# A fused attention, mixture-of-experts and gated-convolution kernel: a re-made instruction list, masks first, half-height masks, divided bursts, tail projections in column halves

## The chip, the core and the metric

The kernel runs on one core of one Trainium2 chip. The time is the device time of one execution in microseconds (us). Several executions are timed and the median is compared. One further execution is taken by the hardware profiler; its trace is the source of every row below. The engines are TensorE (PE, with its weight loads on a track of their own, PEld), VectorE (DVE), ScalarE (ACT), GpSimd (POOL) and SyncE (SP), which here issues the DMAs.

## What is computed

Three stages for 4 batches of 576 positions:

```python
# 1: 8 heads of width 64; heads 0-3 look at the last 32 positions, heads 4-7 at every 32nd
mask_local   = (rel >= 0) & (rel < 32)
mask_strided = (rel >= 0) & (pos[None, :] % 32 == pos[:, None] % 32)
x = softmax(where(mask, q @ k.T / 8, -1e9)) @ v          # laid out as (4, 576, 512)
# 2: 4 experts, each a causal attention of head width 64; a gate keeps 2 of 4 per position
for e in range(4):
    y += gate[e] * (softmax(causal((x @ wq[e]) @ (x @ wk[e]).T / 8)) @ (x @ wv[e]) @ wo[e])
# 3: 512 -> 1024, relu, a 3-tap convolution along positions as gate, 1024 -> 512
h = relu(y @ w_in);  out = (h * sigmoid(conv3(h))) @ w_out
```

## The kernel before

**Number formats.** Products of stages 2 and 3 are made of float16 pairs: each operand is a high part and a low part (what the high part leaves), and `mm3` (L129) issues three products: high by high, low by high, high by low. A low part is made by `low` (L260): TensorE subtracts the high part inside PSUM with a scaled negative identity (`idn`), and ScalarE copies what is left. Stage 1 is in float32, and so is one product of weights: wo and w_in have no nonlinearity between them, so `w_wp` (L747) multiplies them into one matrix `wp` in the prologue (16 float32 products, L758).

**Stage 1** (`s1_local` L297, `s1_strided` L368). One course is a batch's pair of heads: 8 local and 8 strided courses. Each writes its scores by many tiny products (36 of 64x64 for a local, 64 of 64x18 for a strided; in float32 each shows as two records), after two products that lay the mask down (`m_sel` by `m_loc` or `m_str`, L236). A softmax of six DVE steps and one on ACT follows (L243), then a DVE transpose, copies of blocks into block-diagonal tiles (`cp`, L116: one engine each, by the table `ENG`, L71: `bd` alternates ACT and POOL, `bu` is all ACT) and the products with the values (L349, L410).

**Stage 2.** `p_v` (L429) projects the values and the gate's logits, one tile of 128 positions at a time and a last of 64; `p_qk` (L485) projects queries and keys; `a_unit` (L510) is a block of causal attention. It first lays the triangle of the mask into PSUM with two products of full height (`eye` by `m_c`, L521), one for each of two heads; the scores themselves are products of half height (64 rows).

**Stage 3.** `m_gate` (L597) and `m_out` (L633); the last batch ends in `m_last` (L657).

**Order.** All of it is cut into Python generators, one for each piece of work, in nine families: L loads, S stage-1 courses, W weights, O parts of w_out, V, Q, A, M, N. `ORDER` (L38) is a list of 1,669 pairs of letter and number; each pair advances one generator to its next `yield`. The order of the instructions on every engine and queue follows from it, and each engine takes its instructions in that order. The list loop stands under `tc.manual_schedule()` (L809); what comes before it in the function (memsets, masks, identities) is ordered by the framework. All loads go through SP's queue in list order; w_out goes through POOL's.

Of the kernel before, what the change touches and what calls it, by code (L numbers as in the profile page):

```python
# [23 lines left out]
X_S = 2.0 ** 5  # L24
# [9 lines left out]
PF_BUFS = 4  # L34
ST_BUFS = 4
# [3 lines left out]
    "W0W0W0W0W0L0L0L0L0L0W4W5W4W4W4W4W4S0S0S0W4W4S1W4L1L1L1L1L1S2W0S0S0W3S1W3S0L2S1L2S1S0L2S2S0S0S0S0L0S0W3S2S2L2L2S1"  # L39
    "S3S2W3L0L0W4S3S0S0S1W0S3S1S4S4W2S4S0W1W3W3S2S1S1S1S0S1S3W3S0S1S2W2S0S1S1S1S3S1S4W2S2W2W2W2S4S3W2S2S2S3S0S0S0S4W2"  # L40
    "S0S2S0W2S2S1S1L0L0L0L0S0S1S3W2S3S0W2W2S1S1W2W2W2W1W1W0W1W0S0W1W0W0W2L0S1S0S0L0W2W2W2S0S0S0S0S0W2S1S1S0L0S0S0W1S1"
    "S0V0V0W3V1W2W2W2W2V1V1L0W1S0S1W3L0L0L0L0V1W4W3W3V1S0S0S0W2W0W1W0W2W1W0W0W1L0L0W2W1W1S0S1Q0S0W0S1V1W0L0S0S0S1L0S0"
    "W1W1S1S1W1S0S0S0W0S1W0W0S1O0O1O1O1Q0Q0O0O0O0Q0O1V0O2O4V0S1Q0S1V0S2S2S2L0L0S0S0O1V2V0L0S1O1O0O1V0O2S2O1S2O1V0V1V2"
    "O0V2V2S0S0S1O1Q1Q1Q1Q1O6Q1Q0V2S0S0O0Q0Q0S1S0V1Q0V2S0S0A0A0A1A1Q0S0S0S0A0A0V2V2O4A0O1O1A1A1A0L0L0Q0A1A0A0O0S0S0A2"
    "S0V0A2A1A1S0S0Q0Q0A0A0A1O1A4V1A1A1A2O0A2A1A4A4V2A3O0A2A4A3Q0V0V1V1O1V1O0A4A2A0Q0Q0V0A2A2A4A1A1S0O1A3V0A4A2S1A2A2"
    "S0A1A2A0A2A3A0S0A3L1L1A2L1A2A2A2Q0A0Q0A2Q0A1Q0A2A0Q0Q0A2A2A2V0A0A0S1Q0A2A2A1A0S0A3V0O0V1A2L0A2A3A3S0O2A2L1L1A3V0"
    "V1V1S0A2A2A3S0A4A4V0A2A3V0V0S0V0S0L0A5S0A0S1S0A1Q0A2A2A2A0A3S0A5A4A1A3A4A1A2A2Q0S0Q0A0A1V0A3A2A3A4S2A2A2L0A0O1A3"
    "A3V0S1A2A2A2A4A4S2S2A4L0A0S0S0Q0A3A3A4A4S2S1Q2A0Q0Q2S1A3A3A3S0Q0A0V1S0Q0S1V0A3S0S0S0A2A2S1S0S0S0Q1S0S0S0S0Q0Q0V1"
    "O0Q0Q0O1V0Q0A3S1A3S0S0Q0A2A2O1O1Q0O0S0S0S0A4Q0V0A4A4A3O1A3A4Q0S1A2S1Q1V0S0O0V0V0L0O0Q0A0L0Q1L0S1Q0Q0O0O0S0S0A0S0"
    "S1O0O1A0V0A3A1A2A2Q0Q0A3O0A3A2O0S0A1A1S0A3A1A1A2A0O0A0Q0Q0A0A0S0A0S0A2A2O1O0O0M0M0A2A2M0M0M0M0M0S0A2A2M0S0M1O0S0"  # L50
# [820 lines left out]
```

## Time and profile before

| | us |
|---|---|
| median of 3 runs | 386.27 |
| their range | 385.08 to 389.83 |
| the profiled execution | 391.51 |
| its span, first to last instruction | 389.8 |

The profile names for each instruction its start, its length, the line, the operation and the tiles; in brackets stands how long the engine had been idle and what ended that. "issue" there means that the engine waited for nothing that the profile shows. PE's lengths overlap (products are pipelined), so the spacing of starts tells the cost of one. [...]

### The profile page before, as it was taken

The numbers are of one execution on the slowest core, as the hardware profiler recorded it, in microseconds if no ns is written. First come the engines' busy times: TensorE is split into PE (matmuls) and PEld (weight loads), VectorE is DVE, ScalarE is ACT, GpSimd is POOL, SyncE is SP. The second block draws the span as 40 slices with busy tenths as digits, with TensorE's granted clock in tenths as the row PEclk, the third lists the DMA queues.
The fourth block names the chain that finished last, engine by engine and source line by source line (L and its number), as shares of the span: only waits on it lengthen the run. The fifth ranks groups of instructions, "written<-read, shape, count | busy, mean of one in ns | idle before, by whom it ended". The sixth has DMA issues, their size and how long they took to land.

```text
span 389.8 us, 12020 instructions
## 1 busy us (share of the span) xinstructions
PE 355.6 (91%) x4948; PEld 237.4 (61%) x4948; DVE 304.5 (78%) x706; ACT 283.0 (73%) x643; POOL 30.4 (8%) x81
## 2 busy tenths in 40 slices
PE   3249998799999799999999899999999999999994
PEld 2236565666677567777556667777454687655442
DVE  7979996789889679999977766988957489848730
ACT  3357856689899589999587689988875788556532
POOL 4312113020001101000101010000000000000000
PEclk9759999699999889999999999999999999999999
DMA  8993876732955903324874582115169460010004
GB/s 281 323 245 102 225 249 173 279 111 56 222 119 112 137 9 119 78 41 97 202 128 95 116 129 67 29 21 84 33 154 161 121 129 16 0 69 29 0 2 149
DMA packets 79207, 45.91 MB, mean 118 GB/s; under 512 B 63792, under 2 KB 72496, under 8 KB 79152
## 3 DMA queue, kind: packets, MB, share of 16 engines
q1 hardware_dynamic: 78000, 40.94, 44.8%
q0 software_dynamic: 1152, 4.19, 3.0%
q8 instruction: 39, 0.64, 0.7%
q14 instruction: 16, 0.13, 0.1%
HBM read 25.20 MB, written 4.72 MB: 77 GB/s over the span
## 4 chain that ended last, share of the span: by engine, by line
PE 77%; issue 6%; DMA 6%; ACT 6%; DVE 3%; SPq 1%; ACTq 0%; POOLq 0%
PE o L650 14%; PE zav L584 6%; PE oe L650 5%; PE asc L526 5%; PE psq L130 4%; PE psq L131 4%; PE psq L132 4%; PE hps L130 4%; PE hps L132 3%; PE hps L131 3%; PE wps L758 3%; DMA apt<-pn 3%; PE av L349 3%; PE psv L130 2%; PE scs L240 2%
## 5 line engine op out<-in xcount | busy, mean ns | idle before, releaser
L650 PE MATMUL o<-wout,hs 128*128 128x512 f16 x288 | 66.1, 380 | 0.0
L650 PEld LDWEIGHTS <-hs 128*128 128x128 f16 x384 | 36.0, 98 | 42.5 <-issue 1.8
L619 DVE SCALAR_TENSOR_TENSOR t<-hs,taps,t 128x576 f32<-128x576 f32 x64 | 49.4, 818 | 6.9 <-ACT t L124 6.9
L124 ACT ACTIVATE pn<-apf,aden 64x64 f16<-64x64 f32 (+4 forms) x80 | 42.2, 558 | 12.4 <-DMA apt<-pn 6.9
L570 DVE SCALAR_TENSOR_TENSOR pn<-apf,aden,pn 128x320 f16<-128x320 f32 (+4 forms) x80 | 42.5, 549 | 7.5 <-ACT pn L124 7.3
L130 PE MATMUL psq<-xt,wqk 128*128 128x288 f16 x128 | 38.0, 297 | 0.0
L131 PE MATMUL psq<-xt,wqk 128*128 128x288 f16 x128 | 37.7, 295 | 0.0
L132 PE MATMUL psq<-xt,wqk 128*128 128x288 f16 x128 | 37.7, 295 | 0.0
L130 PE MATMUL hps<-z,wp 128*128 128x288 f16 x128 | 36.8, 288 | 0.0
L131 PE MATMUL hps<-z,wp 128*128 128x288 f16 x128 | 36.6, 286 | 0.0
L132 PE MATMUL hps<-z,wp 128*128 128x288 f16 x128 | 36.6, 286 | 0.0
L550 ACT ACTIVATE apf<-asc,anm 64x64 f32<-64x64 f32 (+3 forms) x64 | 29.8, 470 | 5.4 <-DVE anm L535 2.6
L584 PE MATMUL zav<-apt,v 128*64 128x128 f16 (+2 forms) x720 | 30.8, 221 | 1.4 <-ACT ob L124 1.0
L584 PEld LDWEIGHTS <-v 128*64 128x64 f16 (+1 forms) x720 | 22.7, 108 | 11.5 <-issue 7.2
L534 DVE TENSOR_REDUCE anm<-asc 64x2 f32<-64x128 f32 (+3 forms) x32 | 21.8, 681 | 6.1 <-PE asc L526 5.9
L124 ACT ACTIVATE qk<-psq 128x576 f16<-128x576 f32 x32 | 20.3, 641 | 8.5 <-PE psq L132 4.5
L127 DVE TENSOR_TENSOR hs<-t,hs 128x1152 f16<-128x1152 f32 x16 | 21.6, 1352 | 5.5 <-ACT hs L124 5.5
L124 ACT ACTIVATE t<-hs,taps 128x576 f32<-128x576 f32 x32 | 23.7, 772 | 1.0 <-DVE hs L127 1.0
L124 ACT ACTIVATE hs<-t 128x1152 f16<-128x1152 f32 x16 | 18.7, 1171 | 7.3 <-DVE t L625 7.3
L625 DVE SCALAR_TENSOR_TENSOR t<-t,hs 128x1152 f32<-128x1152 f32 x16 | 21.6, 1352 | 3.0 <-ACT t L623 2.9
L611 ACT ACTIVATE hs<-hps 128x576 f32<-128x576 f32 x32 | 20.4, 644 | 4.6 <-POOL hs L610 3.6
L130 PE MATMUL psv<-wvg,xt 128*128 128x260 f16 (+1 forms) x80 | 23.0, 287 | 0.0
(156 smaller groups left out, 786.2 us busy)
## 6 DMA issues: line engine op xcount, KB each, us to landing
st<-in_dram SPq DMA_DIRECT2D x8, 512.0 KB
ow<-in_dram POOLq DMA_DIRECT2D x8, 512.0 KB, 5.2
out_dram<-ob SPq DMA_DIRECT2D x16, 256.0 KB
ul<-in_dram SPq DMA_DIRECT2D x12, 288.0 KB
ul<-in_dram SPq DMA_DIRECT2D x12, 252.0 KB
vs<-in_dram SPq DMA_DIRECT2D x16, 144.0 KB
vn<-in_dram SPq DMA_DIRECT2D x8, 256.0 KB
st<-in_dram SPq DMA_DIRECT2D x4, 386.0 KB
```

The costliest lines, as they stand in the source:

```text
L124: act.activation(out=out, in_=in_, func=ACTF.Copy, scale=scale)
L127: eng.tensor_tensor(out=out, in0=a, in1=b, op=ALU.subtract)
L130: nc.tensor.matmul(out=out, lhsT=ah, rhs=bh, start=first, stop=False)
L131: nc.tensor.matmul(out=out, lhsT=al, rhs=bh, start=False, stop=False)
L132: nc.tensor.matmul(out=out, lhsT=ah, rhs=bl, start=False, stop=last)
L534: dve.tensor_reduce(out=nm[:, 0], in_=asc[:rows, :, :w], axis=mybir.AxisListType.X, op=ALU.max)
L550: act.activation(out=pfs[par], in_=scs[par], func=ACTF.Exp, scale=C2, bias=nm[:, 0, par:par + 1], accum_out=den[:, par:par + 1])
L570: dve.scalar_tensor_tensor(out=pn[:, 1, :w], in0=pfs[par], scalar=den[:, par:par + 1], in1=pn[:, 0, :w], op0=ALU.mult, op1=ALU.subtract)
L584: nc.tensor.matmul(out=av[64 * par:64 * par + 64, 0:rows], lhsT=v2[a][:kk, kb, D * e:D * e + D], rhs=pts[par][:kk, l, kb], start=(kb == 0 ...
L619: dve.scalar_tensor_tensor(out=t_[:, i], in0=tap, scalar=w, in1=t_[:, i], op0=ALU.mult, op1=ALU.add)
L625: dve.scalar_tensor_tensor(out=t_, in0=t_, scalar=1.0, in1=hs[:, :, 1:S + 1], op0=ALU.add, op1=ALU.mult)
L650: nc.tensor.matmul(out=ps, lhsT=g[a], rhs=wout[l][:, f], **at)
```

## The change

1. **The list** is made again (1,739 pairs); the whole function, prologue included, stands under `manual_schedule`, so masks and memsets come in the order in which they are written. The copies of the masks to the upper half are moved up behind each mask; the zeroing of the spare stage-1 set moves from DVE to POOL.
2. **Divided bursts.** The scores of a course may be left after every 8 jobs (`SCORES`), and the local products with the values after blocks 1 and 3 (`SPLIT_AV`).
3. **Half-height masks.** The triangle in `a_unit` is laid by products of 64 rows, one pair for each 64 columns.
4. **Tail projections in column halves.** The last tile of `p_v` (64 positions) is 24 products of half the columns, the two halves on the two halves of TensorE's columns.
5. **Low parts** of some pieces are made by one DVE instruction from PSUM instead of a product and an ACT copy (table `LOW`: 4 of 16 in x, 2 of 16 in q and k, 6 of 16 in v, and the 4 tails).
6. **wo by w_in** in float16 pairs: 48 products instead of 16 float32 ones; each of the 8 pieces, and wo, is split by one ACT and one DVE instruction.
7. **Engine table.** 53 of the 96 block copies go to POOL (32 before), and one of 16 `gl`.

```diff
+SCORES = 8
+SPLIT_AV = (2, 4)
 ORDER = (
...
-ENG = {'bd': 'AP', 'bu': 'A'}
+LOW = {
+    "x": "IIIIIIIIIIIVVVVI",
+    "q": "IIIIIIIIIIIIVIVI",
+    "v": "VIIVIIIIIIIIIIIVVVVI",
+}
+ENG = {
+    "bn": "APPPPAPAAAPAAPPAPAPPAPPPPAAPAAPP",
+    "bu": "APAPAAAAAPAPAPPPAAPPAPAPPPPPPAPP",
+    "bs": "PAPAPAAPAAAAAPAPAPPPAPPPPPAAAPPP",
+    "gl": "VVVVVPVVVVVVVVVV",
+}
...
 def moe_stack_kernel(ctx, tc, qk_in, vloc, vstr, w_p, wo_t, w_in, conv_w, w_out, out):
     nc = tc.nc
+    ctx.enter_context(tc.manual_schedule())
...
         for x in (set_["pp"], *set_["bd"], set_["bs"]):
-            dve.memset(x.bitcast(U32), 0)
+            (gp if n else dve).memset(x.bitcast(U32), 0)
...
-        for row, nr, c0, cw, q, k in jobs:
+        for n, (row, nr, c0, cw, q, k) in enumerate(jobs):
+            if n and n % SCORES == 0:
+                yield
...
+    def low(kind, n, lo, hi, ps, scale, parts):
+
+        if LOW[kind][n] == "V":
+            yield
+            for o, i, h in ((lo, ps, hi),) if len(ps.shape) < 4 else ((x[:, q] for x in (lo, ps, hi)) for q in range(2)):
+                dve.scalar_tensor_tensor(out=o, in0=i, scalar=scale, in1=h, op0=ALU.mult, op1=ALU.subtract)
+            return
...
         for g in range(NG + 1):
+            if g in SPLIT_AV:
+                yield
...
+            ps = bank("psv")
+            half = E * D // 2 + E
+            cols = [slice(0, E * D // 2), slice(E * D // 2, E * D + E)]
+            for kk in range(KD):
+                for i, (x, l) in enumerate(((xh, 0), (xl, 0), (xh, 1))):
+                    for n, c in enumerate(cols):
+                        nc.tensor.matmul(out=ps[64 * n:64 * n + 64, 0:c.stop - c.start], lhsT=x[:, kk, ts],
+                                         rhs=wvg[l][:, kk, c], start=kk == 0 and i == 0, stop=kk == KD - 1 and i == 2)
...
-                for par in range(2):
-                    nc.tensor.matmul(out=scs[par][:, w - rows:w], lhsT=eye[:, :rows], rhs=m_c[:, MZ:MZ + rows],
-                                     start=True, stop=True, skip_group_check=True)
+                for h in range(rows // 64):
+                    for par in range(2):
+                        half = slice(64 * par, 64 * par + 64)
+                        nc.tensor.matmul(out=scs[par][:, w - rows + 64 * h:w], lhsT=eye[half, h, :rows],
+                                         rhs=m_tri[half, h, 64 * h:rows], start=h == 0, stop=True, skip_group_check=True)
...
     def w_wo():
+        woT = stg.tile([128, KD, E * D], F32, tag="st", bufs=ST_BUFS, name="st")
         nc.sync.dma_start(out=woT, in_=wo_t.rearrange("(k p) n -> p k n", p=128))
-        if False:
-            yield
+        yield
+        copy_a(wo2[0], woT, W_S)
+        yield
+        dve.scalar_tensor_tensor(out=wo2[1], in0=woT, scalar=W_S, in1=wo2[0], op0=ALU.mult, op1=ALU.subtract)
...
+        copy_a(w2[0], wi, W_S)
+        yield
+        dve.scalar_tensor_tensor(out=w2[1], in0=wi, scalar=W_S, in1=w2[0], op0=ALU.mult, op1=ALU.subtract)
+        yield
...
-            nc.tensor.matmul(out=wps[hf][:, r], lhsT=woT[:, kk, 128 * r:128 * r + 128], rhs=wi,
-                             start=kk == 0, stop=kk == KD - 1)
+            mm3(wps[hf][:, r], *(x[:, kk, 128 * r:128 * r + 128] for x in wo2), *w2, kk == 0, kk == KD - 1)
```

## Rows read from the trace of the kernel before

**Rows 1.** The page's first line, and its list of DMA queues: instruction fetches.

```profile
span 389.8 us, 12020 instructions
...
q8 instruction: 39, 0.64, 0.7%
```

**Rows 2.** Windows by stage; the columns are named in the first row.

```profile
core 0: us, PE busy (x) PEld busy (x) DVE busy (x) ACT busy (x) POOL busy (x), PEclk, DMA share, GB/s
0.00:30.00 30.00, 11.63 (x512) 8.95 (x514) 24.12 (x52) 12.17 (x23) 9.59 (x25) 0.73 0.92 277
30.00:45.60 15.60, 15.03 (x209) 8.97 (x208) 15.15 (x31) 12.52 (x24) 3.56 (x7) 0.97 0.55 140
45.60:66.70 21.10, 20.44 (x396) 13.86 (x395) 17.27 (x34) 13.23 (x29) 4.46 (x9) 1.00 0.69 211
66.70:75.40 8.70, 5.23 (x38) 4.02 (x37) 6.56 (x15) 5.33 (x11) 0.61 (x2) 0.61 0.98 378
75.40:131.90 56.50, 54.74 (x985) 39.77 (x983) 49.41 (x145) 49.70 (x137) 5.11 (x13) 1.00 0.56 120
131.90:140.30 8.40, 6.02 (x54) 3.87 (x52) 4.69 (x20) 4.87 (x14) 0.00 (x0) 0.59 0.52 73
140.30:378.70 238.40, 236.51 (x2732) 155.29 (x2731) 187.25 (x414) 181.98 (x403) 7.08 (x26) 1.00 0.38 79
378.70:389.80 11.10, 6.03 (x36) 2.65 (x34) 0.00 (x0) 3.23 (x6) 0.00 (x0) 0.99 0.36 132
```

**Rows 3.** Timeline of PE around its idle times, start us and length us first.

```profile
13.96 0.66 PE L240 MATMUL scs<-us 64*18 64x18 f32 x55 [2.27 <-issue]
14.54 0.30 PE L236 MATMUL scs<-m_str,m_sel 64*128 64x144 bf16 x2
14.78 0.80 PE L240 MATMUL scs<-us 64*18 64x18 f32 x71
...
21.52 0.69 PE L240 MATMUL scs<-us 64*18 64x18 f32 x57 [5.95 <-issue]
...
27.17 0.42 PE L240 MATMUL sc<-ul 64*32 64x64 f32 x3 [3.35 <-issue]
...
45.58 0.27 PE L130 MATMUL psv<-wvg,xt 128*128 128x260 f16 x1
...
70.20 0.21 PE L349 MATMUL av<-pv,vn 128*64 128x32 f32 x1 [3.47 <-issue]
...
96.63 0.34 PE L240 MATMUL sc<-ul 64*32 64x64 f32 x15 [0.18 <-issue]
...
134.31 0.35 PE L240 MATMUL scs<-ul 64*18 64x18 f32 x27 [2.38 <-issue]
```

**Rows 4.** Chain that ended last: float32 weight products, output products, output's last tile.

```profile
58.47 3.43 PE wps L758 x8
...
222.37 5.29 PE o L650 x24
...
359.82 0.80 PE o L653 x12
```

**Rows 5.** Timeline, first and last of a tail projection's 12; then all mask products.

```profile
112.67 0.30 PE L130 MATMUL psv<-wvg,xt 128*64 128x260 f16 x1
...
113.91 0.27 PE L132 MATMUL psv<-wvg,xt 128*64 128x260 f16 x1
...
L521 PE MATMUL asc<-m_c,eye 128*128 128x128 bf16 (+1 forms) x64 | 8.7, 217 | 0.0
```

**Rows 6.** Windows, whole span, DVE alone (busy third): tiles sp, pp, wi; line L735.

```profile
0.00:389.80 389.80, 26.27 (x32) 0.96 0.49 118
0.00:389.80 389.80, 17.18 (x34) 0.96 0.49 118
0.00:389.80 389.80, 18.48 (x32) 0.96 0.49 118
0.00:389.80 389.80, 5.27 (x8) 0.96 0.49 118
```

More of the change, by code (lines that the diff above doesn't have):

```diff
@@ L116, in cp @@
     def cp(kind, j, out, in_):
-        e = ENG[kind][j % len(ENG[kind])]
+        e = ENG[kind][j]
         if e == "A":
@@ L308, in s1_local @@
         sc = banks("sc")[:, :, 0:NL]
-        s1_scores(sc, m_loc, [job(g, j) for g in range(NG + 1) for j in range(4 if g < NG else last // 32)])
+        yield from s1_scores(sc, m_loc, [job(g, j) for g in range(NG + 1) for j in range(4 if g < NG else last // 32)])
         done["l", b] += 1
@@ L361, in s1_local @@
         yield
-        yield from low(lo, av[:, 0:S], X_S, [(hi[:, c], av[:, c]) for c in (slice(0, 512), slice(512, S))])
+        yield from low("x", 4 * b + p, lo, hi, av[:, 0:S], X_S, [(hi[:, c], av[:, c]) for c in (slice(0, 512), slice(512, S))])
     def x_tiles(b):
@@ L378, in s1_strided @@
         sc = banks("scs")[:, :, 0:NRES]
-        s1_scores(sc, m_str, jobs)
+        yield from s1_scores(sc, m_str, jobs)
         done["s", b] += 1
@@ L391, in s1_strided @@
         pp = got[0]
-        lp_ = take("lp", b == 0 and p == 1)
+        spared = b == 0 and p == 1
+        lp_ = take("ls" if spared else "lp", spared)
         lp = lp_[:, 0:512]
@@ L422, in s1_strided @@
         yield
-        yield from low(lo, av, X_S, [(hi[:, q], av[:, q]) for q in range(2)])
+        yield from low("x", 4 * b + 2 + p, lo, hi, av, X_S, [(hi[:, q], av[:, q]) for q in range(2)])
     st = {}
@@ L439, in p_v @@
         ts = slice(128 * t, 128 * t + rows)
-        ps = bank("psv")[:rows, 0:E * D + E]
-        for kk in range(KD):
-            mm3(ps, xh[:, kk, ts], xl[:, kk, ts], wvg[0][:, kk], wvg[1][:, kk], kk == 0, kk == KD - 1)
+        if t < NG:
+            ps = bank("psv")[:, 0:E * D + E]
+            for kk in range(KD):
+                mm3(ps, xh[:, kk, ts], xl[:, kk, ts], wvg[0][:, kk], wvg[1][:, kk], kk == 0, kk == KD - 1)
+            parts = [(ps[:, 0:E * D], slice(0, E * D))]
+            lgp = ps[:, E * D:]
+        else:
+            ps = bank("psv")
+            half = E * D // 2 + E
+            cols = [slice(0, E * D // 2), slice(E * D // 2, E * D + E)]
+            for kk in range(KD):
+                for i, (x, l) in enumerate(((xh, 0), (xl, 0), (xh, 1))):
+                    for n, c in enumerate(cols):
+                        nc.tensor.matmul(out=ps[64 * n:64 * n + 64, 0:c.stop - c.start], lhsT=x[:, kk, ts],
+                                         rhs=wvg[l][:, kk, c], start=kk == 0 and i == 0, stop=kk == KD - 1 and i == 2)
+            parts = [(ps[64 * n:64 * n + 64, 0:E * D // 2], slice(E * D // 2 * n, E * D // 2 * n + E * D // 2)) for n in range(2)]
+            lgp = ps[64:128, E * D // 2:half]
         yield
         sc = V2_S / PR_S
-        copy_a(v2[0][:rows, t], ps[:, 0:E * D], sc)
-        copy_a(lg[:rows, t], ps[:, E * D:], 1.0 / PR_S)
+        for p, c in parts:
+            copy_a(v2[0][:rows, t, c], p, sc)
+        copy_a(lg[:rows, t], lgp, 1.0 / PR_S)
         yield
-        yield from low(v2[1][:rows, t], ps[:, 0:E * D], sc, [(v2[0][:rows, t], ps[:, 0:E * D])])
+        if t < NG:
+            yield from low("v", NT * b + t, v2[1][:rows, t], v2[0][:rows, t], ps[:, 0:E * D], sc, [(v2[0][:rows, t], ps[:, 0:E * D])])
+        else:
+            for p, c in parts:
+                dve.scalar_tensor_tensor(out=v2[1][:rows, t, c], in0=p, scalar=sc, in1=v2[0][:rows, t, c], op0=ALU.mult, op1=ALU.subtract)
     def p_gate(b):
@@ L502, in p_qk @@
         yield
-        yield from low(lo, ps, Q_S / PR_S, [(hi[:, hf], ps[:, hf]) for hf in range(2)])
+        yield from low("q", 4 * b + m, lo, hi, ps, Q_S / PR_S, [(hi[:, hf], ps[:, hf]) for hf in range(2)])
     QB = [(0, 64)] + [(64 + 128 * i, 128) for i in range(NT - 1)]
@@ L689, in moe_stack_kernel @@
     m_c = const.tile([128, MZ + 128], BF16, name="m_c")
-    eye = const.tile([128, 128], BF16, name="eye")
+    eye, m_tri = (const.tile([128, 2, 128], BF16, name=n) for n in ("eye", "m_tri"))
     tri = const.tile([128, E, E], F32, name="tri")
@@ L709, in moe_stack_kernel @@
     wout = []
-    woT = stg.tile([128, KD, E * D], F32, tag="woT", bufs=1, name="woT")
     def f64_word(words, c):
@@ L754, in w_wp @@
         yield
+        w2 = t.rearrange("p n w -> p (n w)").bitcast(F16)
+        w2 = [w2[:, 512 * i:512 * i + 512] for i in range(2)]
+        copy_a(w2[0], wi, W_S)
+        yield
+        dve.scalar_tensor_tensor(out=w2[1], in0=wi, scalar=W_S, in1=w2[0], op0=ALU.mult, op1=ALU.subtract)
+        yield
         if kk == 0:
@@ L808, in moe_stack_kernel @@
     }
-    with tc.manual_schedule():
-        for kind, k in zip(ORDER[::2], ORDER[1::2]):
-            k = int(k, 36)
-            if next(items[kind][k], "end") == "end":
-                items[kind].pop(k)
+    for kind, k in zip(ORDER[::2], ORDER[1::2]):
+        k = int(k, 36)
+        if next(items[kind][k], "end") == "end":
+            items[kind].pop(k)
     assert not any(items.values())
```

97 lines of the change are left out of this document (52 added, 45 removed).

## The prediction

> **What bounds the kernel now.** I read the windows by stage first [rows 2]. From 140.3 to 378.7 us PE is busy for 236.5 of 238.4 us at full clock, while DVE has 51 us to spare and ACT 56: PE sets the pace there, and only less work for PE shortens it. PE is not the limit in four places. In the first 30 us it is busy for 11.6, with DMA at 0.92 of its time and DVE busy for 24.1. In 66.7 to 75.4 and in 131.9 to 140.3 it is idle at first and then runs at a mean granted clock of 0.61 and 0.59. In the last 11 us it waits while results leave.
>
> Next I read the timeline of PE around its idle times [rows 3]. Five of them are ended by "issue": 2.27, 5.95, 3.35, 3.47 and 2.38 us. They have one thing in common. Between the first and the second, PE runs 55 + 2 + 71 = 128 products, each with a weight load of its own: 256 instructions, begun and gone in 1.6 us, and then a gap of 5.95. The counts of the windows add up to some 4,950 products, so 9,900 PE instructions, and the page has 39 instruction packets [rows 1]: 254 instructions a packet. So I take these gaps for PE running out of code: one block of 256 is fetched while the one before it runs. From the start of one block to the start of the next are 21.52 - 13.96 = 7.6 us and 27.17 - 21.52 = 5.65 us with DMA nearly full. At 96.63 the gap is 0.18 us after a run as short, with DMA at work for little: there a fetch takes about 2 us. A gap is the fetch time less the time that 128 products last.
>
> [...] In 66.7 to 75.4, 3.47 us are idle and the other 5.2 us at half speed, which loses 2.6: 6.1 us. In 131.9 to 140.3 it is 2.38 and half of 6.0: 5.4 us. Together 11.5.
>
> [...]
>
> **Less work for PE.** The prices are those of [rows 4, 5]; an output product of 512 columns takes 5.29/24 = 0.220 us, or 0.43 ns a column.
> wo by w_in: 32 records at 3.43/8 = 0.429 are 13.7 us; after, 48 products of 512 columns at 0.220 are 10.6. Saved 3.1.
> Tails: 12 products from 112.67 to 113.91 are 0.113 each, 1.35 a tail. After, 12 pairs in column halves: at best half, 0.68; the nearest row, output's last tile in column halves, has 0.80/12 = 0.067 for a record, 0.133 for a pair of 256 columns where 0.11 would be ideal, so I add that 0.02 to each pair: 0.95. Saved 0.4 to 0.67 each, I take 2.0 for four.
> Masks: a block of 128 rows needs 128 + 64 columns for both heads instead of 256, one of 64 rows 64 instead of 128. By columns that is 64 x 0.43 ns x 32 blocks = 0.9 us. At most it is half of the 8.7 us that all mask products are busy, 4.3. I take 1.2, near the columns.
> Low parts: 4 x 576 + 2 x 576 + 10 x 256 = 6,016 columns fewer, 2.6 us. DVE gets them instead; nearly all lie in batches 2 and 3, under its 51 spare us.
> Sum: 3.1 + 2.0 + 1.2 + 2.6 = 8.9, between 7 and 13.
>
> **The two later gaps.** I counted both lists in runs of 128 products, at the prices of these rows. Behind the prologue the old list has four runs under 3 us, all of them scores: the two that end in the rows at 70.20 and 134.31, the one of 96.63, and one that shows no gap. The new list has none; its shortest are 5.0, 3.9, 5.4, 5.4, 4.1, 5.8, 5.7 and 3.9 us, since a course's scores now stand in two or more parts with projections or attention between them. Against a fetch of 5.65 us each time, what is left of gaps is 0.65 + 1.75 + 0.25 + 0.25 + 1.55 + 0 + 0 + 1.75 = 6.2 us; against 2 us, nothing. I take 3, without loss of clock, in place of 11.5.
>
> **The prologue.** Masks first brings the first scores forward by a us or so, which code and DVE then eat up. The bursts are divided in the list, but here the next entry is mostly another course's burst: 826 products stand before the first product of wo and w_in, where 518 stood. That is 2.4 blocks more, 13 to 18 us at 5.65 to 7.6, if DMA stays full. It will not: in the new order wp00, wo and wproj3 share four buffers and wait for DVE to finish earlier weights, and the strided load of batch 1 waits for the local scores of batch 1.
>
> So I follow DVE. Per course, local work is 26.27/8 = 3.28 on tile sp, plus the maximum and two small steps, about 1.25 (estimate: the maximum reads the same 640 elements as a quarter of the 3.28): 4.5. Strided: about 2.9 from 17.18/8 = 2.15 and the same additions at half size. Weights: 18.48/8 = 2.31 for a piece of w_in, 5.27/4 = 1.32 for a piece of the projections [rows 6]. Up to the last split of wproj3 and the last strided transpose of batch 0, the new list puts on DVE: three local courses 13.5, two strided 5.8, two steps of a fourth 1.7, four projections 5.3, w_in 2.31 + 0.9, wo 1.2 (estimate: 1,024 elements, twice a step of w_in), small ones 0.5: 31 us. They start with the first scores, near 8 us. The blocks must then be copied, multiplied, split and subtracted, some 3.7 us: first projection at 43 us if DVE never waits; at the busy share of 39.3/45.6 that DVE has before [rows 2], 48. I take 46. Before, it is 45.58 [rows 3], so nothing seems lost; but the old list has done five of the eight pieces of wo by w_in by then and the new one only one, plus one more strided course. Four pieces at 6 x 0.220 less 1.3 are 4.0 us behind. From 45.6 to 131.9 PE has too little slack to get that back [rows 2]. Bounds: 0 (43 us) to 8 (50 us, or blocks at 5.65).
>
> **At nothing.** More block copies on POOL, which is busy for 0.08 of the span by the sums of [rows 2], and one `gl`: ACT and DVE gain what they lose. The splits of w_in and wo are in the sum for DVE above, the rest of them (seven at 18.48/32 = 0.6 or so [rows 6]) go on beside projections; if DVE were the limit from 46 to 75 us, they would cost up to 5 (third rival). The last 11 us stay.
>
> **Sum.** Against the profiled execution, 391.5 (span 389.8 [rows 1] and 1.7 around it): 391.5 - 8.9 - 11.5 + 3 + 4 = 378.1. That execution is 5.2 us above the median of 386.3. If the 5.2 are longer gaps of the kind that goes away, the median saves less and ends at 378; if they are spread evenly, at 373. I forecast **376 us**.
>
> **Rivals.**
> 1. Gaps come back elsewhere or the prologue lags by 8: only the cut in work is left. 391.5 - 8.9 - 11.5 + 6.2 + 8 = 385.3 by the profile, 380 to 385 by the median. For it: eight runs under 6 us, 308 more narrow products early on. Against it: none under 3.9.
> 2. The gaps are not PE's code but another hold that comes with full DMA (0.98 in 66.7 to 75.4 [rows 2]). Then dividing does nothing: 391.5 - 8.9 + 4 = 386.6, 381 to 387 by the median. [...]
> 3. DVE is the limit from 46 to 190 us: 75.4 to 131.9 already has 49.4 of 56.5 busy. Five to eight us more: 383 to 386.
> 4. Slower: the short gaps take the clock with them. Each of the two rows lost 2.6 to 3.0 us to half clock after a gap of 2.4 to 3.5. Eight gaps that each did so would cost 6.2 + 8 x 2.8 = 28.6 instead of 3: 403.7, 398 to 404. It decides from six of them on, about 395. Against it: gaps of 0.2 to 1.8 are shorter than any that did it here.
>
> **How the numbers follow.** Forecast 0.55 (own range 368 to 381), rival 1 0.18, rival 2 0.06, rival 3 0.10, rival 4 0.11. Within 2% of 386.3 (378.5 to 394) is about what a measurement of this kernel can't tell from no change. Of the forecast 0.45 of the 0.55 lies below 378.5, with 0.07 of rivals 1 and 3 at their favourable ends: faster 0.52. Slower is rival 4 above 394, and some of rival 1 with both bounds at their worst: 0.12. The rest, 0.36, is the same. The range for 8 in 10 leaves out rival 4 and the lowest end: 367 to 391.
>
> **What would show it.** Right: no gap by "issue" over 2 us after 50 us, and a clock of 1.00 from 75 us to the end; first psv or psq near 46 us; wps near 10.6 us in all; tails near 0.95; 140 us to the end shorter by some 6 us. Wrong: a fetch gap over 2 us with the clock at half behind it (rival 4), PE waiting for DVE between 46 and 75 us (rival 3), or a first projection later than 50 us.

## The result, and the profile after

| | median us | lowest to highest | ratio to before, 95% interval |
|---|---|---|---|
| before, 12 runs beside it | 388.05 | 384.99 to 392.25 | |
| after, 12 runs | 382.40 | 380.96 to 384.38 | 0.9876 [0.9844, 0.9908] |

The change makes the kernel 1.24% faster, between 0.9 and 1.6%. The forecast was 376 us, 2.7% under the median shown then: right in direction, less than half as large. The profiled execution of after took 384.26 us. (Ratios, here and below, leave out executions that were disturbed, so they need not be the quotient of two medians.)

The page's first lines, kernel after:

```profile
span 382.5 us, 12229 instructions
...
PE 345.0 (90%) x5038; PEld 229.1 (60%) x5038; DVE 313.4 (82%) x733; ACT 273.5 (72%) x619; POOL 51.1 (13%) x110
```

Windows by stage, kernel after, with the columns of [rows 2] (PEclk is the share of TensorE's full clock that was granted):

```profile
0.00:30.50 30.50, 13.31 (x572) 9.38 (x574) 25.30 (x56) 13.73 (x27) 16.17 (x36) 1.00 0.96 263
30.50:46.70 16.20, 12.11 (x268) 8.79 (x265) 14.39 (x26) 11.25 (x21) 4.24 (x7) 0.79 0.78 195
46.70:80.70 34.00, 34.00 (x584) 24.14 (x583) 28.91 (x62) 23.33 (x52) 8.15 (x13) 1.00 0.57 167
80.70:91.60 10.90, 4.21 (x54) 2.92 (x52) 6.65 (x17) 5.66 (x11) 2.72 (x7) 0.61 0.77 292
91.60:131.90 40.30, 37.39 (x694) 26.67 (x689) 35.92 (x115) 33.97 (x98) 5.49 (x10) 0.98 0.66 113
131.90:160.00 28.10, 26.35 (x483) 19.41 (x478) 26.32 (x78) 22.86 (x64) 5.54 (x14) 1.00 0.60 119
160.00:368.00 208.00, 207.09 (x2352) 133.05 (x2352) 175.97 (x384) 159.49 (x344) 8.75 (x24) 1.00 0.41 79
368.00:382.50 14.50, 10.50 (x64) 4.71 (x58) 0.00 (x0) 3.26 (x6) 0.00 (x0) 1.00 0.27 100
```

Read it against [rows 2]. From 46.7 to 80.7 PE is never idle: the stretch in which the old list had its gap of 3.47 us is full. From 160 to 368 PE is busy for 207.09 of 208 us at clock 1.00. Between them, from 80.7 to 91.6, PE works for 4.2 of 10.9 us, at a clock of 0.61: a hole that the kernel before did not have, and that no step of the prediction names.

Timeline of the kernel after, all engines, in order of time (start us, length us, engine, line, idle time before and what ended it):

```profile
13.42 1.54 PE L258 MATMUL scs<-us 64*18 64x18 f32 x128 [2.27 <-issue]
19.34 0.34 PE L258 MATMUL scs<-us 64*18 64x18 f32 x25 [4.38 <-issue]
27.18 0.25 PE L258 MATMUL scs<-us 64*18 64x18 f32 x3 [5.45 <-issue]
...
44.57 0.61 PE L145 MATMUL wps<-st,wo 128*128 128x512 f16 x1
...
46.75 0.33 PE L145 MATMUL psq<-xt,wqk 128*128 128x288 f16 x1
...
78.23 2.61 POOL L845 DMA_DIRECT2D ow<-in_dram  x5 [6.06 <-issue]
...
84.04 1.22 ACT L766 ACTIVATE oc<-ow 128x512 f32<-128x512 f32 x2 [7.01 <-DMA ow<-in_dram]
...
84.73 0.43 DVE L768 TENSOR_SCALAR oc<-oc 128x512 f32<-128x512 f32 x1 [7.14 <-ACT oc L766]
...
86.14 0.63 ACT L139 ACTIVATE qk<-psq 128x576 f16<-128x576 f32 x1
...
86.82 0.64 PE L286 MATMUL psq<-qk,idn 128*128 128x288 f16 x2 [5.86 <-ACT qk L139]
...
88.29 2.19 PE L436 MATMUL avs<-bs,vs 128*64 128x72 f32 x32 [0.83 <-ACT qk L139]
```

The last six rows are the hole. POOL issues five loads of w_out's parts, part 1's first among them, only at 78.23 us. By the program they go into memory that the weights' staging buffers hold till then; the row itself names nothing that ended POOL's wait. In the new list the first step of part 1 (ACT takes the absolute value of the high word, L766) stands right behind six of these loads, and ACT comes to it before the load is even issued. It stands still for 7.01 us until the data has landed; the copy of a projection (L139) that stands behind in the list starts only at 86.14 us, and PE waits 5.86 us for it. DVE waits 7.14 us in the same place. In the old list, where two loads stand ahead of it, ACT waited in its own first step of w_out too, for 3.6 us. Rows of the kernel before:

```profile
63.08 1.59 POOL L785 DMA_DIRECT2D ow<-in_dram  x3 [8.73 <-DVE pp L257]
...
67.15 1.22 ACT L716 ACTIVATE oc<-ow 128x512 f32<-128x512 f32 x2 [3.61 <-DMA ow<-in_dram]
```

### The profile page after: what moved, and what is told of

Same layout as the page of the kernel before. It is cut to its first block, busy times and chain, and to the rows that moved or that the text cites. A ratio compares the mean times of both kernels' runs of the same rounds, so it can differ in the third digit from the quotient of the medians.

```text
span 382.5 us, 12229 instructions
## 1 busy us (share of the span) xinstructions
PE 345.0 (90%) x5038; PEld 229.1 (60%) x5038; DVE 313.4 (82%) x733; ACT 273.5 (72%) x619; POOL 51.1 (13%) x110
## 4 chain that ended last, share of the span: by engine, by line
PE 64%; DVE 12%; DMA 10%; ACT 8%; issue 5%; SPq 1%; POOL 0%; ACTq 0%; POOLq 0%; DVEq 0%
PE o L697 16%; DMA st<-in_dram 6%; PE oe L697 6%; PE zav L631 5%; PE hps L145 4%; PE hps L147 4%; PE hps L146 4%; PE asc L573 3%; PE o L700 2%; PE psq L145 2%; PE psq L146 2%; PE psq L147 2%; PE avs L436 2%; DVE pn L617 2%; PE av L374 2%
## 5 line engine op out<-in xcount | busy, mean ns | idle before, releaser
L617 DVE SCALAR_TENSOR_TENSOR pn<-apf,aden,pn 64x64 f16<-64x64 f32 (+4 forms) x80 | 43.4, 551 | 6.0 <-ACT pn L139 5.3
L139 ACT ACTIVATE pn<-apf,aden 64x64 f16<-64x64 f32 (+4 forms) x80 | 41.9, 558 | 8.4 <-DVE aden L606 2.2
L145 PE MATMUL psq<-xt,wqk 128*128 128x288 f16 x128 | 36.8, 287 | 0.0
L147 PE MATMUL psq<-xt,wqk 128*128 128x288 f16 x128 | 36.6, 286 | 0.0
L146 PE MATMUL psq<-xt,wqk 128*128 128x288 f16 x128 | 36.6, 286 | 0.0
L631 PE MATMUL zav<-apt,v 128*64 128x128 f16 (+2 forms) x720 | 31.6, 221 | 1.4 <-DVE z L640 1.1
L142 DVE TENSOR_TENSOR hs<-t,hs 128x1152 f16<-128x1152 f32 x15 | 20.3, 1352 | 10.0 <-ACT hs L139 9.8
L658 ACT ACTIVATE hs<-hps 128x576 f32<-128x576 f32 x32 | 20.8, 650 | 10.3 <-PE hps L147 6.8
L136 POOL COPY bn<-lp 32x320 f32<-32x320 f32 x34 | 19.9, 584 | 44.7 <-PE av L374 24.8
L139 ACT ACTIVATE hs<-t 128x1152 f16<-128x1152 f32 x16 | 18.6, 1161 | 8.0 <-DVE t L672 8.0
L139 ACT ACTIVATE t<-hs,taps 128x576 f32<-128x576 f32 x32 | 23.4, 771 | 0.0
L670 ACT ACTIVATE t<-t 128x1152 f32<-128x1152 f32 x16 | 18.6, 1161 | 5.7 <-DVE t L666 5.6
```

The lines of the kernel that those rows point to most:

```text
L139: act.activation(out=out, in_=in_, func=ACTF.Copy, scale=scale)
L145: nc.tensor.matmul(out=out, lhsT=ah, rhs=bh, start=first, stop=False)
L146: nc.tensor.matmul(out=out, lhsT=al, rhs=bh, start=False, stop=False)
L147: nc.tensor.matmul(out=out, lhsT=ah, rhs=bl, start=False, stop=last)
L617: dve.scalar_tensor_tensor(out=pn[:, 1, :w], in0=pfs[par], scalar=den[:, par:par + 1], in1=pn[:, 0, :w], op0=ALU.mult, op1=ALU.subtract)
L631: nc.tensor.matmul(out=av[64 * par:64 * par + 64, 0:rows], lhsT=v2[a][:kk, kb, D * e:D * e + D], rhs=pts[par][:kk, l, kb], start=(kb == 0 ...
```

## The experiments

Gains are given against the kernel before, run beside each on the same chip (medians 388.2 to 388.8). A difference between two changed kernels is one of medians, mostly from two chips and from 4 to 12 executions each; by the intervals it is good to 2 to 3 us.

### The wait for w_out

**e1_late_o**: the kernel after with nine list entries moved: those of w_out's parts 0 and 1 behind the loads. Numbers are places in the list.

```diff
-354 O1 abs, 355 O1 clamp, 357 O0 abs, 362 O1 combine, 366 O1 combine, 376 O0 clamp, 393 O0 combine, 401 O1 copy, 412 O0 combine
+404 to 412: the same nine, in the same order
```

> The changed kernel with one edit of the list: the nine steps of w_out's parts 0 and 1 that follow their loads are moved some 50 entries on, behind the projections and courses that stood behind them. Theory W (ACT stands in order behind the loads of w_out, and PE waits for ACT): the idle time of 5.9 us at 80.7 us and the half clock after it go, some 8 us in all; about 374 us, ratio to the kernel before 0.965. Rival D (DVE is the limit between 47 and 160 us, the wait only shows it): at most 2 us, 380 us or more.

Measured: 378.93 us, ratio 0.9799 [0.9748, 0.9849]. The 5.86 us are gone, but the nine steps now stand in a bunch, and in it PE waits for an ACT copy once more:

```profile
89.01 0.38 PE L145 MATMUL psv<-wvg,xt 128*128 128x260 f16 x1 [2.86 <-ACT v L139]
```

So half of the loss comes back; the rest was either this bunch or DVE.

**e6_spread_o**: the same idea with the steps apart (places in the list of the kernel after).

```diff
-354 O1 abs, 355 clamp, 362 combine, 366 combine, 401 copy, 453 subtract
+405 O1 abs, 412 clamp, 421 combine, 431 combine, 438 copy, 453 subtract
-357 O0 abs, 376 clamp, 393 combine, 412 combine, 427 copy, 431 subtract
+446 O0 abs, 456 clamp, 466 combine, 476 combine, 484 copy, 497 subtract
-440 O4 abs, 448 clamp; 369 load of O5; 419 load of O2
+499 O4 abs, 506 clamp; 432 load of O5; 478 load of O2
```

> The kernel after with the steps of three w_out parts (1, 0, 4) later in the list and spread out, about ten entries between two steps of a part, and the sixth and seventh load's turn behind the step that frees their buffer. In the run with the steps only later, they stood in one bunch, and PE still waited 2.9 us for an ACT copy behind them. Theory W (a w_out step that stands ahead of its time in ACT's order is all that the new list loses at 80 to 91 us): 375 to 377 us, ratio about 0.972, PE busy for over 8.5 of the 10 us from 80 to 90. Rival D (DVE is the limit from 80 to 160 us, so that the work left over only moves): 378 to 380 as with the bunch, the idle time shows up between 100 and 160 us instead.

Measured: 375.55 us (374.77 to 377.2), ratio 0.9659 [0.9595, 0.9724]: the best kernel of this study, 6.9 us below the kernel after (8.4 by the two ratios). Theory W holds. The step that stood for 7 us in ACT now starts without a wait, between two softmax steps:

```profile
85.02 0.19 ACT L597 ACTIVATION_READ_ACCUMULATOR apf<-asc,anm 128x1 f32 x1
85.11 0.66 ACT L766 ACTIVATE oc<-ow 128x512 f32<-128x512 f32 x1
85.67 0.51 ACT L597 ACTIVATE apf<-asc,anm 128x320 f32<-128x320 f32 x1
```

Nothing but the order changed: the same instructions, 3.4% faster than before where the kernel after was 1.2%.

### Is DVE the limit from 80 to 160 us?

**e7_no_unpack**: the spread kernel without the DVE instructions that unpack w_out (by the program four a part, where the expectation says five).

```diff
-        yield from f64_word(t, c)
+        act.activation(out=c, in_=t[:, :, 1].bitcast(F32), func=ACTF.Abs)
+        yield
...
```

> As the spread kernel of this call, but the five DVE instructions that unpack each part of w_out (clamp, shift, two combinations) are left out, for all eight parts: DVE has some 18 us less to do between 85 and 160 us, and ACT waits for DVE in none of these steps. The copies to float16 and the subtractions stay. Rival D (DVE limits 90 to 160 us): 4 to 5 us shorter than the spread kernel, PE busy for over 9.8 of 10 us in each stretch from 90 to 160. Theory W (only the place of the first steps counts): within 1.5 us of the spread kernel.

Measured: 373.12 us (371.83 to 373.97), ratio 0.9601 [0.9545, 0.9657], 2.4 us below the spread kernel. One window of 80 to 160 us, first of the kernel after:

```profile
80.00:160.00 80.00, 68.65 (x1235) 49.69 (x1232) 68.88 (x207) 62.49 (x170) 14.45 (x32) 0.94 0.66 142
```

The same of the spread kernel:

```profile
80.00:160.00 80.00, 73.21 (x1293) 53.88 (x1291) 73.84 (x213) 70.17 (x184) 13.37 (x30) 1.00 0.77 155
```

And without the unpacking:

```profile
80.00:160.00 80.00, 75.56 (x1406) 56.13 (x1405) 62.57 (x188) 69.58 (x186) 11.06 (x25) 0.98 0.75 150
```

PE's idle time (80 less the first number) goes from 11.4 to 6.8 to 4.4. DVE does 11.3 us less in the last window than in the second, and its share of the loss is that last step, 2.4 us: between the two ways of the expectation. The third rival of the prediction is there, but, as far as this kernel shows it, with 2.4 us and not 5 to 8.

### The fetch gaps, the divided bursts and the prologue

**e2_whole**: the kernel after with each burst issued whole at its first list entry.

```diff
         for n, (row, nr, c0, cw, q, k) in enumerate(jobs):
-            if n and n % SCORES == 0:
-                yield
             for par in range(2):
...
+        for n in range(SCORES, len(jobs), SCORES):
+            yield
```

> The changed kernel with the same list, but a course's score products are all issued at its first step (the divided steps stay in the list and issue nothing). Theory C (PE runs out of code when 128 products are short): the strided courses of batches 2 and 3 again stand as 128 short products in a row; one or two gaps of 2 to 3.5 us come back behind 60 us, each with half clock after it, 4 to 10 us in all; 386 to 392 us. Rival H (the gaps of the kernel before were another hold that comes with full DMA, or the change avoids them by its order alone): no gap ended by issue behind 50 us, 382 us as the changed kernel.

Measured: 382.86 us, ratio 0.9892 [0.9832, 0.9952], no difference from the kernel after, and no wait by "issue" above 0.7 us behind 50 us. In the new order even whole bursts make no gap: other products stand close enough around them. Counted in blocks of 128 products, none behind the prologue is gone in less than 4.2 us here, where the block ahead of the gap at 70.20 us of the kernel before is gone in 2.2. In none of the nine traces of kernels with the new list is there a gap by "issue" of over 1.3 us behind 50 us. It is the order that took the gaps away; the division adds nothing to it.

**e10_split_two**: the kernel before, with the division alone, and only for the two bursts ahead of the later gaps of [rows 3].

```diff
-256 S7 scores x128 (strided, batch 1, head pair 1)
+217, 241, 242, 246: S7 scores x32 each, behind wps or projection products
-591 S11 scores x128 (strided, batch 2, head pair 1)
+582, 594, 605, 609: S11 scores x32 each, behind projection products
```

> The kernel before with two bursts of scores divided into four parts of 32 products each, with entries of projections or wps between them: the strided scores of batch 1, head pair 1, begun some 60 list entries earlier, and those of batch 2, head pair 1. Nothing else is changed. These are the bursts ahead of the fetch gaps of 3.47 and 2.38 us. Theory of the prediction (a block of 256 PE instructions that is gone before the next has come): the block before each gap lasts 4 to 5 us in place of 1.9 and 2.6, the gaps shrink to some 1.3 and 0.9 us, the half clock behind them goes: 3 to 5 us shorter, ratio 0.990. Rival (a hold that comes with full DMA, wherever the products stand): the gaps stay at 2 us or more, ratio 1.000. Third way: the gaps shrink but PE is not the limit from 66 to 140 us: ratio 0.997 to 1.000 without the gaps.

Measured: 387.33 us, ratio 0.9967 [0.9923, 1.001]. Timeline of PE, the first quarter of both bursts, the products at which the kernel before has its gap of 3.47 us, and the one gap left:

```profile
62.32 0.32 PE L242 MATMUL scs<-ul 64*18 64x18 f32 x32
...
67.54 0.26 PE L351 MATMUL av<-pv,vn 128*64 128x32 f32 x4
...
76.63 1.22 PE L412 MATMUL avs<-bs,vs 128*64 128x72 f32 x32 [1.00 <-issue]
...
128.84 0.32 PE L242 MATMUL scs<-ul 64*18 64x18 f32 x32
```

In this trace the gaps of 3.47 and 2.38 us are gone, and so is the half clock: the window of 66 to 144 us has a clock of 1.00, where that of before has 0.91:

```profile
66.00:144.00 78.00, 71.59 (x1229) 52.77 (x1228) 67.33 (x198) 66.19 (x178) 6.30 (x16) 1.00 0.63 147
```

The same window of the kernel before:

```profile
66.00:144.00 78.00, 70.39 (x1178) 51.27 (x1175) 62.87 (x184) 62.25 (x167) 6.42 (x16) 0.91 0.58 141
```

This alone does not show that the division did it. e13 (below) has the same divided bursts, and its first 1,112 products are those of e10 in the same order; its trace has a gap of 1.56 us inside a quarter of the burst and one of 2.19 us at the product where the kernel before has 3.47. And e15 (below), undivided and with the products of the kernel before in the same order up to there, has 0.25 us at the product where that one has 2.38:

```profile
130.50 0.31 PE L240 MATMUL scs<-ul 64*18 64x18 f32 x27 [0.25 <-issue]
```

What a gap waits for stands in another record of the traces, the packets of the instruction queue (39 of 16,384 bytes each, [rows 1]). PE goes on soon after one has landed:

| kernel | gap ends at, us | last packet before it has landed at | PE goes on after |
|---|---|---|---|
| after | 13.42 | 11.90 | 1.52 |
| after | 27.18 | 25.63 | 1.55 |
| before | 70.20 | 68.76 | 1.45 |
| e13 | 64.53 | 62.81 | 1.72 |
| e13 | 70.55 | 69.04 | 1.51 |
| before | 134.31 | 130.62 | 3.69 |

In the seventeen traces 71 gaps of over 0.7 us by "issue" stand at an edge between blocks of 128 products, and 69 of them end 1.25 to 1.73 us behind the landing of a packet. So they are PE's code coming late, as the prediction has it, and the second rival is out for the gap at 70.20. The two others are the one at 134.31 and the same one in e5: their packet had landed before PE stopped, and what held PE there stays open. When a packet comes differs between executions: while the block of 128 products that begins at some 57 us runs, the next packet starts 4.5 us behind the block's begin in the kernel before, 5.0 us in e13 and 1.6 us in e10. A block that lasts longer leaves room for a packet as late as these; whether a short one leaves a gap is partly chance.

The time follows the third way of the expectation: only 1.3 us (between 0 and 3) come out. PE is idle for 6.4 of these 78 us instead of 7.6: in e10's trace it waits for ACT and DVE there (1.25 us for a copy of ACT at 69.06 us, 0.62 for another at 98.94, 0.43 for DVE at 94.22). The full price of gaps and half clock this is not, because the clock of e10's twelve executions lies between 0.966 and 1.000, so in most it still fell somewhere. But the half clock at least does not show as dear: the four executions at 0.997 or more took 383.2 to 388.2 us, and over the 89 executions of the kernel before that ran beside these experiments the time hardly follows the clock (correlation -0.22).

One block of 256 instructions is enough for a gap: the rows at 13.42 and 19.34 us of the kernel after have one at each end of a single block. Behind the prologue of that kernel no block is gone in less than 3.9 us, and there is no gap by "issue" above 0.7 us.

**e5_masks_first**: the kernel before with the new prologue alone (masks first, memory clearing divided between POOL and DVE, whole list in the listed order).

```diff
-            dve.memset(x.bitcast(U32), 0)
+            (gp if n else dve).memset(x.bitcast(U32), 0)
...
+    ctx.enter_context(tc.manual_schedule())
```

> The kernel before with the prologue of the change alone: the whole function under the written order, masks first with their copies behind them, the spare set zeroed on POOL. As predicted: first scores some 2 us earlier, but PE then waits for code and DVE, so the first projection stays at 45 to 46 us and the time within 1 us of the kernel before. Rival (the first scores set the prologue's end): 2 to 3 us faster.

Measured: 387.44 us, ratio 1.0021 [0.9974, 1.0067]: nothing. Its profiled execution still has both later gaps, with a granted clock of 0.989 over the whole span where the profiled execution of before had 0.960:

```profile
69.22 0.19 PE L351 MATMUL av<-pv,vn 128*64 128x32 f32 x1 [2.11 <-issue]
...
132.14 0.34 PE L242 MATMUL scs<-ul 64*18 64x18 f32 x27 [2.20 <-issue]
```

### What the cuts in PE's work are worth

First in the new list, one cut undone at a time. **e4_low_pe** undoes the low parts in the kernel after, **e12_spread_low_pe** in the spread kernel:

```diff
-    "x": "IIIIIIIIIIIVVVVI", "q": "IIIIIIIIIIIIVIVI", "v": "VIIVIIIIIIIIIIIVVVVI",
+    "x": "IIIIIIIIIIIIIIII", "q": "IIIIIIIIIIIIIIII", "v": "IIIIIIIIIIIIIIIIIIII",
```

> The kernel after with all low parts back on PE and ACT (the table of low parts all I), but for the tails. PE gets 6,016 columns more, 2.6 us, and ACT the copies; DVE loses as many steps, nearly all in batches 2 and 3. If PE alone sets the pace from 160 us on: 2.6 us longer than the kernel after, 385, ratio 0.994. If DVE were the limit there: no change or up to 2 us shorter. A step that stood well in the list on DVE may stand badly on ACT: up to 3 us more.

> The spread kernel with all low parts but the tails' back on PE and ACT. The same edit on the kernel after cost 5.9 us, where columns say 2.6. If the rest was ACT's copies in the way (ACT stood in the chain where PE waited for its copies after 160 us): again 5 to 6.5, 381 to 382. If it came from the wait for w_out, which the spread kernel does not have: 2.6, 378.

Measured: 388.61 us (ratio 1.0028 [0.9991, 1.0065]), 6.2 more than the kernel after; and 382.23 us (0.986 [0.9817, 0.9904]), 6.7 more than the spread kernel. The columns account for 2.1: PE gets 18 products of 4,992 columns (the 6,016 of the expectation count the tails, which these runs leave alone). Much of the rest is in the waits of PE behind 160 us, spread kernel with low parts on PE and ACT:

```profile
PE avs L286 <- ACT xt L139: 1.5, 2, 1.2
PE psv L286 <- ACT lg L139: 0.7, 1, 0.7
PE asc L573 <- ACT qk L139: 0.6, 1, 0.6
PE psq L145 <- ACT qk L139: 0.4, 1, 0.4
PE psq L286 <- ACT qk L139: 0.3, 1, 0.3
```

These 3.5 us are waits for ACT's copies; in the spread kernel itself the same view shows none for ACT over 0.2. A low part on PE cost its products here, and waits of PE for ACT's copies.

**e9_old_tails_masks** undoes tails and masks, **e11_spread_wps32** the float16 products of wo and w_in:

```diff
+        for kk in range(KD):
+            mm3(ps, xh[:, kk, ts], xl[:, kk, ts], wvg[0][:, kk], wvg[1][:, kk], kk == 0, kk == KD - 1)
...
+                    nc.tensor.matmul(out=scs[par][:, w - rows:w], lhsT=eye[:, :rows], rhs=m_c[:, MZ:MZ + rows],
+                                     start=True, stop=True, skip_group_check=True)
```

```diff
-            mm3(wps[hf][:, r], *(x[:, kk, 128 * r:128 * r + 128] for x in wo2), *w2, kk == 0, kk == KD - 1)
+            nc.tensor.matmul(out=wps[hf][:, r], lhsT=woT[:, kk, 128 * r:128 * r + 128], rhs=w32,
+                             start=kk == 0, stop=kk == KD - 1)
```

> The spread kernel (the list of after with the steps of three w_out parts later and apart) with two cuts undone: last tiles of the projections in 12 products again and full masks. By the rows of the run with these cuts in the old list they take 2.5 and 3.9 us of PE's work away there, and the time did not move. If the new list lets PE set the pace, undoing them costs the whole 6.4: 382 us, ratio 0.982. If the cuts are covered by other engines in this list too: 375 to 377, ratio 0.967.

> The spread kernel with wo by w_in in float32 again: 32 products instead of 48 of float16, wo and the pieces of w_in not split (the ACT step of a piece stays as a plain copy, DVE's eight subtractions and one for wo go). By rows, PE gets 13.7 to 15.6 us of products in place of 10.3: 3.4 to 5 us more before 70 us; DVE has some 5 us less there. If PE sets the pace from 45 to 80 us in the new list: 379 to 380.5. If DVE does, as the third rival of the prediction had it: 373 to 375.5, no longer than the spread kernel.

Measured: 380.3 us (0.98 [0.9759, 0.9841]), 4.8 more than the spread kernel, of 6.4 in the expectation; and 381.47 us (0.9842 [0.9795, 0.9889]), 5.9 more. Each cut pays in this list. The 5.9 are more than the 3.4 to 5 that the rows explain, but by less than these runs can tell; the profiled execution of that kernel was its fastest, 379.19, and shows no place for a rest.

Then the same cuts put into the old list. **e3_cuts_only** has all four, the new steps of the split standing in the list entry of the product that needs them:

```diff
+        copy_a(w2[0], wi, W_S)
+        dve.scalar_tensor_tensor(out=w2[1], in0=wi, scalar=W_S, in1=w2[0], op0=ALU.mult, op1=ALU.subtract)
         if kk == 0:
             wps[hf] = banks("wps")
```

> The kernel before, with its own list, order of prologue and engine table, and four parts of the change: tails in column halves, half-height masks, low parts on DVE by the table, wo by w_in in float16 pairs. Theory as predicted (PE is the limit, so less work for PE is saved in full): 7 to 13 us, forecast 8.9; 379 us, ratio 0.977. Rival D (DVE is the limit until 160 us, and the splits of w_in and wo add 6.5 us to it): only what lies behind 140 us is saved, 3 to 5 us; 384 us, ratio 0.99.

Measured: 407.83 us, ratio 1.0505. Waits of PE behind 46 us:

```profile
PE wps L135 <- ACT st L129: 9.5, 3, 7.4
PE psv L463 <- ACT v L129: 2.6, 1, 2.6
```

The split of a piece stands right ahead of its product and goes through ACT, behind whatever ACT waits for: 9.5 us in three waits. Of some 19 us lost these rows hold 12. This run says nothing on the cuts' size, and much on the place of a step. **e3b_pe_cuts** leaves it out: tails and masks alone.

> The kernel before with two of the cuts alone, those that put nothing new on ACT before 80 us: last tiles of the projections in column halves (with their low part on DVE) and masks from half-height matrices. By the sum of the prediction 2.0 + 1.2 = 3.2 us shorter than before; by the first mask rows of the profile after (0.05 us a product where 0.10 stood) masks may save up to 3: 5 us shorter in all. If PE's work were not the limit from 140 us on: no change.

Measured: 388.27 us, ratio 1.0063 [1.0025, 1.0101] (the medians lie 0.6 us apart the other way): no gain. Yet its timeline shows both cuts, larger than forecast:

```profile
99.17 0.26 PE L543 MATMUL asc<-m_tri,eye 64*128 64x128 bf16 x4
99.26 0.25 PE L548 MATMUL asc<-qk 64*128 64x192 f16 x2
...
104.76 0.27 PE L263 MATMUL psv<-v,idn 128*128 128x256 f16 x1 [1.61 <-ACT lg L124]
...
110.63 0.88 PE L453 MATMUL psv<-wvg,xt 128*64 128x128 f16 x24
111.45 0.30 PE L548 MATMUL asc<-qk 64*128 64x288 f16 x2
```

The mask products of a block of 128 rows take 99.26 - 99.17 = 0.09 us where before they take 0.22 (103.22 to 103.44); a tail 111.45 - 110.63 = 0.82 where it is 1.45 (112.67, the first row of [rows 5], to the next product at 114.12). With 24 blocks of 128 rows at 0.13, eight of 64 rows at 0.13 (0.05 for 0.18) and four tails at 0.63 that is 6.7 us of PE's work. The windows show where it went:

```profile
66.00:144.00 78.00, 66.93 (x1230) 49.19 (x1227) 65.74 (x193) 64.55 (x171) 5.56 (x14) 0.98 0.68 140
160.00:387.40 227.40, 218.35 (x2534) 137.67 (x2530) 168.04 (x377) 165.40 (x363) 5.27 (x21) 1.00 0.38 81
```

PE is idle for 11.1 of the 78 us, where the kernel before has 7.6, and behind 160 us for 9.1, where before has 6.9 (222.89 busy of 229.80). The work became waiting: 1.61 us for a copy of ACT in the rows above, and short waits by "issue".

Three runs asked what covers the cuts there. **e13_split_cuts** joins the two bursts divided with these cuts; **e14_cuts_no_unpack** and **e15_before_no_unpack** leave DVE's unpacking out, with the cuts and without. Their edits are those of e10, e3b and e7.

> The kernel before with the two bursts divided (which left no fetch gap above 1 us and gained 1 us) and with tails in column halves and half-height masks (which alone gained nothing). If the gaps and the clock after them had eaten the gain of the cuts: 6 us or more less than the run with the bursts divided, 381, ratio 0.981. If other engines cover the cuts from 66 to 160 us: 386 to 388, ratio 0.995 to 1.000.

> The kernel before with tails in column halves and half-height masks, and with the five DVE instructions that unpack each part of w_out left out for all eight parts: some 18 us less for DVE between 66 and 160 us. If DVE's work there covered the cuts: 5 to 7 us less than the next kernel of this call, which leaves out the same but has no cuts. If it did not: within 1.5 us of it.

> The kernel before with the same five DVE instructions a part of w_out left out, nothing else. In the list after, with its steps spread, this gave 2.4 us. If DVE sets the pace from 66 to 160 us in the old list: 3 to 6 us less than before, ratio 0.985 to 0.992. If PE does: ratio 0.997 to 1.000.

Measured: 390.15 us (1.0029 [0.9992, 1.0066]), 387.58 (0.9977 [0.9937, 1.0016]) and 388.53 (0.9978 [0.9941, 1.0016]). DVE's work isn't the cover: 15.8 us less of it over the span (e15), 10.6 of them between 66 and 160 us, move the old list by nothing, with the cuts or without. And e13 (by the medians 2.0 us longer than before, by the interval the same) could not answer, because its trace has gaps again. The first two are at edges that e10 has too, with the same products ahead of them, and come with late packets (table above); at the third the added products have put other work at the edge:

```profile
64.53 0.32 PE L242 MATMUL scs<-ul 64*18 64x18 f32 x31 [1.56 <-issue]
...
70.55 0.19 PE L351 MATMUL av<-pv,vn 128*64 128x32 f32 x1 [2.19 <-issue]
...
119.72 0.21 PE L608 MATMUL zav<-apt,v 64*64 64x64 f16 x1 [1.35 <-issue]
```

What covers the cuts in the old list stays open. That single relieves (prologue, divided bursts, DVE, PE's work) each move it by at most 1.3 us, while the new list answers to the two that were tried there, DVE's and PE's work, is what the runs show.

## Why the prediction was right and wrong

**Right.** The gaps are code (for the one at 134.31 us that is open), and the new order has none over 2 us behind 50 us; its shortest block of 128 products behind the prologue lasts 3.9 us, as the prediction had counted. First projections stand at 46.75 and 47.53 us (forecast 46). A piece of wo by w_in is six products from 65.81 to 67.10 us, 0.215 each, 10.3 in all (forecast 10.6). From 160 us on PE is at full clock and never long idle. Rival 4 did not occur, the second is out for the gap at 70.20 us, and the third is there with 2.4 us (e7).

**Two more signs.** From 140 us to the end it is 242.5 us where 249.8 were (forecast some 6 less). But these 7.3 us are the whole difference of the two spans, so they hold what was won and lost ahead of 140 us as well and don't tell. The clock, the other sign, came out wrong: it is not 1.00 from 75 us to the end but 0.61 in the hole, behind a wait for ACT and not behind a gap of the kind foreseen.

**Wrong, the gaps' price.** "Together 11.5", less 3, took the idle time and the half clock of two gaps as time lost at the end. The half clock is in that trace: 0.50 from 69.0 to 75.4 us and from 134.3 to 140.3. Dividing the two bursts brought 1.3 us in the old list (e10). Two things failed. The 11.5 come from one execution, and its clock of 0.960 is not that of most runs: of the runs of before beside e6, one took 386.3 us at a clock of 0.970, one 387.1 at 0.995, one 390.4 at 0.984; the time hardly follows the clock. And the step from "PE is idle here" to "the kernel is longer by this" needs PE to be the limit in that stretch. The first part of the prediction had said that from 66.7 to 140 us PE is not the limit in two places; it then priced both at full.

**Wrong, the cuts' price.** 8.9 us was the sum of columns. Undone one at a time in the spread list they cost 4.8 (tails and masks, forecast 3.2), 6.7 (low parts without the tails, 2.1) and 5.9 us (wo by w_in, 3.1), each good to some 3 us. Masks were the term most off: 4.2 us of work by the rows of e3b, where I took 1.2 "near the columns" although my upper bound was 4.3. The low parts bring more than columns; 3.5 us of it are waits for copies that leave ACT, a gain that the prediction did not count. The three don't add up to what the change brought; a step undone also stands wrong in a list made for the other way.

**Wrong, the missing step.** The sum had no term for where the list puts w_out. ACT's first step stands right behind six loads, where two stood; ACT comes to it at 77.03 us, the load that it needs goes out only at 78.23, PE stands for 5.86 us, and 6.9 us are lost (after against e6). The rule to look at what is queued behind a waiting instruction was applied to the prologue and not to this list entry, although the old list had the same wait, 3.6 us long, in the same place.

**Prologue: open.** The arrears that the term of 4 us prices are there. Up to 45.6 us the new kernel has issued 3 of its 48 products of wo by w_in; the old one had issued 16 of 32 records, four of the eight pieces (the prediction says five). From 30.5 to 46.7 us PE is busy for 12.11 us at a clock of 0.79. That PE is full from 46.7 to 80.7 us does not say that the arrears were made up, and no run prices them: e5 has the new masks with the old list. The lag of 8 us of rival 1 is not there, with first projections at 46.75 us.

That the spread kernel takes the 376 us of the forecast is chance: the terms differ.

## What to carry to other kernels

Idle time of PE is worth its length only in a stretch where PE is the limit; price a gap by what the next engine would then hold up, and by several executions, not one. In a list that fixes the order on every engine, look for every step that waits for a DMA and ask what stands behind it: moving fifteen list entries was worth more here than the whole change. A cut in work was worth nothing here until the order was made for it: measure cut and order together, and then look at the first hole in the new timeline.

## What the runs showed of the hardware

The gaps of code fell at fixed counts of instructions, not at fixed work: in the kernel after, the second gap comes exactly 128 products (256 instructions with their weight loads) behind the first, all of one kind, and the old list, with other work in another order, has its first gaps the same 128 products apart (55 + 2 + 71, [rows 3]). Products added early on put other work at a later edge (the gap of e13 at 119.72 us, 1.35 us long).

Such a gap ended 1.25 to 1.73 us behind the landing of a packet of 16,384 bytes in the instruction queue (69 of 71 gaps in seventeen traces); the gap at 134.31 us of the kernel before, 3.69 us behind one, has a further cause that no run shows. The block ahead of the gap of 3.47 us was gone in 2.2 us; in the kernel after, where no block behind the prologue is gone in less than 3.9, no such gap is above 0.7. When the packet comes counts as well: at one and the same product, with the same products ahead of it, e13 has 2.19 us and e10 none.
